# VectorE turns x in 32×32 squares from batch 2 on; folded weights lie by batch in DRAM

## The chip, the core and the metric

One core of a Trainium2 chip runs the whole program. The metric is the device time of one execution in microseconds (us); lower is better. TensorE is called PE here, VectorE DVE, ScalarE ACT, SyncE SP (as in the profile). Every DMA of this kernel is issued by SP, in program order.

## The reference, cut to what matters

```python
# x (8, 8, 512, 64), state (8, 8, 32, 64): batch, head, position, depth
scores  = x @ state.T / 8;   a  = softmax(scores);   xread = a  @ state
scores2 = state @ x.T / 8;   a2 = softmax(scores2);  sread = a2 @ x
t = concat([xread, sread], axis=2)        # 8 * (512 + 32) tokens of 512 values
h = (t @ w1) * (t @ w2)                   # 512 -> 1024, twice
y = (h @ w3) @ w_out                      # 1024 -> 1024 -> 512
h2 = y @ w_in;  out = (h2 - tanh(h2)) @ w_out2     # 512 -> 2048 -> 512
```

The weights arrive as 64-bit numbers, and are turned to fp32 on the chip.

## The kernel before, in words

**First part (about the first 543 us).** `xread` is never formed: the state of a batch is folded into w1 and w2, so that the attention weights are multiplied with folded weights. Nine blocks of tokens (eight batches of 512, one of 256 `sread` rows) go through these stages:

- *Unpacking* (`unpack_abs`, `unpack_tail`, `unpack_clamp`, `unpack_shift`, `unpack_end`, lines 334 to 369): three DVE and one or two ACT operations per piece of weights. `unpack_tail` is on ACT or DVE.
- *w3 times w_out* (`w3_turn`, `w3_mul`): a product of 16 tiles, at the start.
- *Folding* (`fold`, lines 936 to 952): per group r of four batches, pair kk of 128 columns and quarter q, PE multiplies the turned state `uu` with w1 and w2. `fold_whole`, or `fold_hi` and `fold_lo`, take the result out of PSUM into tiles `fe`; `fold_store` (line 976) writes each half j to DRAM (`mdr`), as rows of 1 KB, one store per r, kk, q, half j and, for r = 1, high and low part l.
- *Attention of batch b* (`attn_parts`). `load_xn` brings x with positions on the partitions, as pieces of 64 values (256 bytes). `turn_x` (line 467) turns one quarter q with four PE transposes into PSUM (`x_ps`); `xt` (line 471) copies it out on ACT; `scores` needs all four `xt`. Then softmax both ways on DVE and ACT (`by_head` and `back` are DVE transposes in 32×32 squares, line 493 and 551), `e2t` (PE transposes), `sread`.
- *First product* (`stage1`, tiles `ab_ps`): for batch b and k of 8, the attention weights times the folded weights `m`. `load_m` (line 1057) fetches `m` with four DMAs of 32 partitions; for r = 0 `m_hi` and `m_lo` split it. `ab_take` (ACT) and `ab_mul` (DVE) multiply the two halves, `ab_hi` (ACT) and `ab_lo` (DVE) split the result into `ph`.
- *Second product* (`stage2`, tiles `y_ps`), `y_take` (ACT) and `y_store`, one tile at a time, to DRAM (`ydr`).
- The second model's weights are fetched (`raw_w`), unpacked, and stored to DRAM (`w2dr`) in the same time.

**Second part (from 543 us to the end).** `stage3` (`h_ps`) and `stage4` (`o_ps`) alternate on PE, twelve matmuls each; the `curve` runs on DVE and ACT. The change doesn't touch this part.

**What sets the order.** `part(...)` describes each step with its engine, an estimated duration, needs and buffers. The string `ORDER` (line 91) has a letter for each step: the letter names a stream and an engine. `Plan.run` emits the steps in that order, so each engine's list, and SP's list of DMAs, is written out by the string. Buffers come from rings: four `xt` (shared with `a` and `e2t`), three `m`, four `fe`, two `at`.

An engine does its list strictly in order: what waits holds up what stands behind it. A stage's tiles `m_ps`, `sc_ps` and `sr_ps` are *tiled* matmuls, which use a part of PE's rows or columns; the others use all of it.

Of the kernel before, what the change touches and what calls it, by code (L numbers as in the profile page):

```python
# [68 lines left out]

ENGINES = ("PE", "ACT", "DVE", "SP")  # L70
LETTERS = "abcdefghijklmnopqrstuvwxyzABCDEFGHIJKLMNOPQRSTUVWXYZ0123"
ORDER = (
    "lllllllljljklklljkljklmklnlkjlqjhkkjkjkqkjkkmjknkkjxqkxxkjlkmkxqnkdjkkkqjkkkmkqnkxjkxxqkxjkmjqkk"
    "mknnkqjkkjqkjekqhkfkvqkvkmkmwxmnmxwjqxwlnxkvxqxvxkxkqwwnqwnrkrersrlafgabhsabmhsbmsavqbwvwaqnwbbe"
    "cncvqcfcbhwqbwvgechcadjcqwjkqkcvqkvcmqccncbwqbwvwmfawqnhwbgbebhjcagafcvehhcqccbkvqcfccvghekhagaF"
    "kfbakbebhhgafFmbwmnenwvhgqhwfvwhehwqwfgHhwHehFIqfIghehKfgHhIheqfghhertLsKfgrhrshKzMrALKMLsazMebA"
    "LagfMKhbshbcKcLcbeFMcLacfObchbdMObgHcheIcafgebhOcbhfcKfcgbKcLcceOcfFgfgOhMhcLehMHhacbaFIfOcfczgh"
    "OghhAKhcHeILafKbghfghKzhMhALKLMezFMAfOFfgLgOHhMhIOhHheIKfFfgKgLhhKzMhLhAKHMLIezMAfKfghLgKhLMhhez"
    "MFAfaabgObhfhzOghLAhHMeIafFabgObfhKghhHhOLIOePPKRfRfhKzFMALKgLgheMhzhMfOFALHMOPghfIRahhbKcbPcKLR"
    "cbcOHFcbMaIObdcLcKbgHchKLcbeccafFcObgfIbOFMcOchchOHMhIHKLIMKLgchKcbFMcLKLMOzMALOHMIaacecafKbghfg"  # L80
    "hKLhhKzMALKLMazFMabAebHaFbaIObffOghLghHMOhhIOaebbcFOfcfgObghhcahcOHhcbIbdKcPRcbKcLcPKFPMPKLccLRR"
    "bMORzcMOALMOKHIKLKzMALKLMaFMebLabaMFfcOfcHOhccOIbcHcOccIKgghheLhafFaObbfgKhghhaMFObLHOMhIKHKLIKF"
    "MLKLMKFMHKLILZMZOFMHOLIMaabKbTKLUUTaFMTUbKUbcZTVcKcbcOLFcbcHOHcdLcOITcOTIPaMPKRMbRUbUKbUVLcZLaFM"
    "KbMPUPUORLZcLVOMbRcHcOIcaTcaTUKUcHcbKUFccOTcIZTUVUKMULOZHMVLIFKMLKLMTKTMFUUKUTZTUOFUOULZLMVOMVaa"
    "bbaababKbLKLMaFMTObUcbTUOcTcObULcZTOVMcbacdObUbcOUUcVOZcbTOcPcPRTKcRUUPUaPRKVLZbRbOFMcLKMcKLcTUK"
    "TFMULaULaMVOZccbOcTccTUOUUaabKZbVKFMLKLMKFMTLUKUTMOTFUTUUOLVUZKMVZLKMLKFMLKLMOFMTOTUUKLUMTZKVLUU"
    "TOFMUOVZKLMKTTUUKFLUOMVZOKTTUUOFLULOMZMVOLTMOTUUPKUPRZPVKLRRPTaFMabUaLUObMRbKTTKULUVTUZOMFUOLVMZ"
    "abObccObccOTcTcaOcdbbcbUOUTUTOcVZUbacKbccbUKLccKFMcKLMLKcTFcTMKULUVMLZObFUMOULMZVOcOKTTUUKLUOFML"
    "aTMaVTccZKUUUaObVLZKPPRKFMLaLMaRbabaObTbUKUPPRTKFMTKULUZLMRTKFMULaULMZVbKVbccKFcbcOcbcaKcbbMcKcb"
    "TacbOcTUOcUbUTOcLVZcLDaTEaMOMcLOcLcbUOcTcTcOUMUaObUZbUVbcOcUOVOKTTUUKMDULKEVLMKDMELOMDLEOOOPPRKR"  # L90
    "PPRRKDMLEKMLDEKDMLEKMDLEKDMLEKMDLEKDMLEKMDLEKDMEKDEKDEKDEOFOOLLMOMKLLMMKFOFOOLLMOM333OL3MOOOOOO1"
    "OP2KPR1R3K2LKFMLKLM3PRKPFMLKLMR1OFM2LKM3K1LO2FMOL3MOOK1KL21KFM2LKLM31KM12LOLM32OO112O123O12O23OK"
    "KMLKLMOMLOMOOPPRRPRPR"
)
# [1376 lines left out]
```

## Time and profile before

| | us |
|---|---|
| three runs | 1290.15, 1293.03, 1292.68; median 1292.68 |
| the profiled execution's own time | 1292.19 |
| its span in the trace | 1290.4 |
| PE busy, share of the span | 1275.8, 99% |
| DVE busy | 966.3, 75% |
| ACT busy | 752.6, 58% |
| DMA queue of SP, share of 16 engines | 35.9% |

The profiled execution is one of its own beside the three runs, 0.49 us below their median, and 1.8 us longer than its span. Busy time of PE includes matmuls whose records overlap: a row "x12 | 2.88 us" spans twelve matmuls that start 0.227 us apart. What a group of matmuls costs on PE is the time from its start to the start of what follows it.

### The profile page before, as it was taken

What the parts mean: (1) busy time and instruction counts of PE and PEld (TensorE: products, weight loads), DVE (VectorE), ACT (ScalarE), POOL (GpSimd) and SP (SyncE); (2) the same over time, 40 slices, a digit from 0 to 9 for tenths busy, and PEclk for the clock granted to TensorE, in tenths of its full rate; (3) what the DMA queues carried; (4) which work ended last, traced back from release to release, by engine and by line L of the source; (5) the groups of instructions that cost most, each with busy time, mean ns of one, the idle gap of its engine ahead of it and who ended that gap; (6) DMA issues with size and microseconds to landing.
All of it is one profiled execution on the core that took longest, in us unless ns stands there. A gap on an engine that the chain in (4) does not pass through costs nothing.

```text
span 1290.4 us, 17503 instructions
## 1 busy us (share of the span) xinstructions
PE 1275.8 (99%) x6420; PEld 1017.4 (79%) x6420; DVE 966.3 (75%) x1602; ACT 752.6 (58%) x1208; POOL 0.7 (0%) x6
## 2 busy tenths in 40 slices
PE   8999999999999999999999999999999999999998
PEld 5436777877888799888888888888888888888887
DVE  7888776586757754499787787776877877768777
ACT  8986666486766754465454454554544545545444
POOL 0000000000000000000000000000000000000000
PEclk9999999999999999999999999999999999999999
DMA  9986774577989627530100100100101001001000
GB/s 337 311 257 193 241 236 146 166 216 214 296 267 243 184 74 235 152 120 1 39 27 1 66 1 1 66 1 29 37 1 66 1 1 66 1 1 50 1 34 17
DMA packets 111365, 141.66 MB, mean 110 GB/s; under 512 B 43440, under 2 KB 81328, under 8 KB 109232
## 3 DMA queue, kind: packets, MB, share of 16 engines
q1 hardware_dynamic: 111280, 140.54, 35.9%
q8 instruction: 51, 0.84, 0.3%
q14 instruction: 34, 0.28, 0.1%
HBM read 89.13 MB, written 51.38 MB: 109 GB/s over the span
## 4 chain that ended last, share of the span: by engine, by line
PE 86%; DMA 5%; DVE 3%; ACT 2%; SPq 2%; issue 1%; DVEq 0%; ACTq 0%
PE h_ps L316 27%; PE o_ps L1394 27%; PE ab_ps L316 14%; PE y_ps L1124 14%; DMA raw_p<-in_moe_w_dram 2%; PE m_ps L941 1%; PE m_ps L948 1%; PE x_ps L308 1%; DMA raw<-in_moe_w_dram 1%; DMA mdr<-fe 1%; SPq L758 1%; DMA m<-mdr 1%; PE w3o_ps L790 1%; SPq L753 1%; DMA w2dr_in<-dt_w 1%
## 5 line engine op out<-in xcount | busy, mean ns | idle before, releaser
L316 PE MATMUL h_ps<-yt,w2in 128*128 128x512 f32 (+1 forms) x1728 | 394.0, 377 | 0.0
L316 PEld LDWEIGHTS h_ps<-yt,w2in 128*128 128x128 f32 x1728 | 313.5, 188 | 61.1
L1124 PE MATMUL y_ps<-ph,w3o 128*128 128x512 f32 (+1 forms) x864 | 197.7, 381 | 0.0
L316 PE MATMUL ab_ps<-at,m 128*128 128x512 f32 x768 | 185.1, 393 | 1.0 <-DMA m<-mdr 1.0
L1124 PEld LDWEIGHTS y_ps<-ph,w3o 128*128 128x128 f32 x864 | 153.7, 188 | 32.4 <-issue 3.1
L316 PEld LDWEIGHTS ab_ps<-at,m 128*128 128x128 f32 x768 | 142.5, 188 | 36.5 <-issue 3.3
L1107 DVE TENSOR_TENSOR ac<-ab_ps,ac 128x512 f32<-128x512 f32 (+1 forms) x72 | 47.3, 657 | 36.8 <-PE ab_ps L316 31.7
L286 ACT ACTIVATE ph<-ac 128x512 fp32r<-128x512 f32 (+1 forms) x72 | 43.8, 609 | 48.4 <-DVE ac L1107 34.0
L289 DVE TENSOR_TENSOR ph<-ac,ph 128x512 fp32r<-128x512 f32 (+1 forms) x72 | 47.4, 658 | 27.2 <-ACT ph L286 25.8
L790 PE MATMUL w3o_ps<-wo,w3t 128*128 128x512 f32 x128 | 59.4, 602 | 3.5 <-ACT w3t L286 2.2
L790 PEld LDWEIGHTS w3o_ps<-wo,w3t 128*128 128x128 f32 x128 | 22.7, 190 | 31.7 <-issue 24.4
L286 ACT ACTIVATE ac<-ab_ps 128x512 f32<-128x512 f32 (+1 forms) x72 | 41.2, 572 | 8.3 <-PE ab_ps L316 8.0
L344 ACT ACTIVATE raw_w<-raw_w 128x512 uint16<-128x512 uint32 x32 | 43.9, 1373 | 0.6
L1404 DVE COPY ob<-o_ps 128x512 f32<-128x512 f32 x17 | 11.8, 692 | 39.1 <-PE o_ps L1394 39.1
L286 ACT ACTIVATE fe<-m_ps 128x512 fp32r<-128x512 f32 (+1 forms) x48 | 28.3, 608 | 18.7 <-PE m_ps L941 8.3
L286 ACT ACTIVATE ob<-o_ps 128x512 f32<-128x512 f32 x17 | 10.2, 599 | 45.1 <-PE o_ps L1394 45.1
L335 ACT ACTIVATE dt_w<-raw_w 128x512 f32<-128x512 f32 x32 | 21.5, 673 | 19.3 <-DMA w2dr_in<-dt_w 9.2
L289 DVE TENSOR_TENSOR m<-m 128x512 fp32r<-128x512 f32 x32 | 21.7, 685 | 14.1 <-ACT m L286 14.1
L286 ACT ACTIVATE m<-m 128x512 fp32r<-128x512 f32 x32 | 19.9, 628 | 20.3 <-DMA m<-mdr 20.1
L289 DVE TENSOR_TENSOR fe<-m_ps,fe 128x512 fp32r<-128x512 f32 x32 | 21.3, 687 | 10.3 <-DMA mdr<-fe 5.4
L368 DVE SCALAR_TENSOR_TENSOR dt_w<-raw_w,dt_w 128x512 uint32<-128x512 uint32 x32 | 22.1, 690 | 7.0 <-ACT raw_w L344 5.8
L355 DVE TENSOR_SCALAR dt_w<-dt_w 128x512 f32<-128x512 f32 x32 | 13.4, 420 | 16.8 <-ACT dt_w L335 14.9
(1826 smaller groups left out, 2347.5 us busy)
## 6 DMA issues: line engine op xcount, KB each, us to landing
mdr<-fe SPq DMA_DIRECT2D x96, 256.0 KB, 2.7
m<-mdr SPq DMA_DIRECT2D x128, 128.0 KB, 4.4
raw<-in_moe_w_dram SPq DMA_DIRECT2D x16, 512.0 KB, 9.4
xn<-in_x_dram SPq DMA_DIRECT2D x8, 1024.0 KB, 8.2
m<-mdr SPq DMA_DIRECT2D x128, 64.0 KB, 2.2
ydr<-y SPq DMA_DIRECT2D x32, 256.0 KB, 4.2
raw_w<-in_moe_w_in_dram SPq DMA_DIRECT2D x16, 512.0 KB, 5.4
raw_w<-in_moe_w_out_dram SPq DMA_DIRECT2D x16, 512.0 KB, 4.9
```

Of the source, the lines that this page charges most:

```text
L286: nc.scalar.activation(dst, src, AF.Copy)
L289: nc.vector.tensor_tensor(out=lo, in0=src, in1=hi.bitcast(F32), op=ALU.subtract)
L308: nc.tensor.transpose(dst[:, i * P:(i + 1) * P], s, ident)
L316: nc.tensor.matmul(out_ap, lhs(i), rhs(j), start=(n == 0), stop=(n == m - 1))
L335: nc.scalar.activation(t.bitcast(F32), word(raw, 1).bitcast(F32), AF.Abs)
L344: nc.scalar.activation(tail, word(raw, 0), AF.Copy, scale=TAIL)
L355: nc.vector.tensor_scalar(out=t, in0=t, scalar1=EXP_LO, scalar2=EXP_HI, op0=ALU.max, op1=ALU.min)
L368: nc.vector.scalar_tensor_tensor(out=t if to is None else to, in0=word(raw, 1), scalar=0xC0000007, in1=t, op0=ALU.bitwise_and, op1=ALU.bit ...
L790: nc.tensor.matmul(acc[a], v[:, a * P:(a + 1) * P], wo[:, j].bitcast(F32), start=(j == 0), stop=(j == nj - 1),)
L1107: nc.vector.tensor_tensor(out=ab[b, k], in0=ab[b, k, 1], in1=ab[b, k], op=ALU.mult)
L1124: nc.tensor.matmul(acc[o][:, :n], w3o[k // 4][:, k // 2 % 2, i, c + o * P:c + (o + 1) * P], p[:, j], start=(k == 0 and e == 0), stop=(k == ...
L1394: nc.tensor.matmul(acc[t], g[:, i, t * P:(t + 1) * P], w[:, l, c], start=(f == 0 and e == 0), stop=(f == NF - 1 and e == 2),)
```

## The change

Eight edits, and an order written anew:

1. From batch 2 on, `turn_x` and `xt` are gone. `squares(q)` loads a quarter of x once more from DRAM, already sorted into 32×32 squares (four DMAs, in runs of 32 values, 128 bytes), and `turn_squares(q)` turns all squares of the quarter in one DVE operation in place. `load_xn` stays, for `sread`.
2. `mdr` is laid out by batch: `[l, b, q, n, k, f]`. The rows of a folded tile are now (n b) instead of (b n), because the copy of `uu` interleaves the four batches.
3. `fe` is one tile of 512×2 for both halves j; `fold_store` stores it with one DMA per r, kk, q and l.
4. `load_m` is one DMA over all 128 partitions.
5. For r = 0 `fold_whole` takes both halves on one engine.
6. `y_take` takes two tiles on one engine and `y_store` stores them with one DMA (except for the last two blocks).
7. `part` has an argument `other`: a second engine for the same step. The string `CHOICE` has a bit for each such step; 1 takes the other engine. It applies to `xt`, `take`, `e2take`, `unpack_tail`, the copies of `w3t` and `uu`, `fold_whole`, `ab_take` and `y_take`.
8. Entries of the cost tables, used to make the order.

```diff
-        (r, kk): dram.tile([KT, P, 2, 2, 512], F32, name=f"mdr{r}_{kk}")
+        (r, kk): dram.tile([2, 4, KT, NS, 2, 512], F32, name=f"mdr{r}_{kk}")
...
+    def move(dst, src, eng):
+        if eng == "ACT":
+            copy(dst, src)
+        else:
+            nc.vector.tensor_copy(dst, src)
...
+            def squares(q):
+                s["xt", q] = pt.tile([P, 512], F32, tag="xt", name=f"xt{b}_{q}", bufs=4)
+                for n in range(4):
+                    j, d = divmod(n, 2)
+                    nc.sync.dma_start(
+                        s["xt", q][n * 32:(n + 1) * 32].rearrange("k (c w i) -> k c w i", c=NC, w=4),
+                        x[b, 2 * q + j, :, d * 32:(d + 1) * 32].rearrange(
+                            "(w k c) i -> k c w i", w=4, c=NC
+                        ),
+                    )
+
+            def turn_squares(q):
+                nc.vector.transpose(out=s["xt", q], in_=s["xt", q])
...
+                if b >= SQUARES:
+                    part(
+                        q_s, "SP", "squares", later(squares, q), [(b - 1, "e2t", j) for j in range(G)],
+                        [(b, "xr", q)],
+                        [("xt", (b, "xt", q))],
+                    )
+                    p("DVE", full, turn_squares, (q,), [("xr", q)], [("xt", q)])
+                    continue
...
-        def fold_store(r, kk, q, j, l):
+        def fold_store(r, kk, q, l):
             nc.sync.dma_start(
-                mdr[r, kk][q, :, :, l, j * 256:(j + 1) * 256], fes[r, kk, q, j, l].bitcast(F32)
+                mdr[r, kk][l, :, q].rearrange("b n k f -> n b (k f)"),
+                fes[r, kk, q, l].bitcast(F32).rearrange("p k f -> p (k f)"),
             )
...
-            for q in range(KT):
-                rows = slice(q * NS, (q + 1) * NS)
-                to = mt[b, k][rows].bitcast(F32)
-                of = mdr[r, k // 2][q, bb * NS:(bb + 1) * NS, k % 2]
-                nc.sync.dma_start(*((to, of) if r else (to[:, 1], of[:, 1])))
+            of = mdr[r, k // 2][:, bb, :, :, k % 2].rearrange("l q n f -> (q n) l f")
+            to = mt[b, k].bitcast(F32)
+            nc.sync.dma_start(*((to, of) if r else (to[:, 1], of[:, 1])))
...
-        def ab_take(b, k, n):
+        def ab_take(b, k, n, eng):
             ab[b, k] = pa.tile([P, 512], F32, tag="ac", name=f"ac{b}_{k}")[:, :n]
-            copy(ab[b, k], ab[b, k, 0])
+            move(ab[b, k], ab[b, k, 0], eng)
...
+            if b < B - 1:
+                nc.sync.dma_start(ydr[b][:, os[0]:os[1] + 1, :], ys[b, os])
...
-    "lllllllljljklklljkljklmklnlkjlqjhkkjkjkqkjkkmjknkkjxqkxxkjlkmkxqnkdjkkkqjkkkmkqnkxjkxxqkxjkmjqkk"
+    "ppppppppnpnopoppnopnopqopsnpopnopuohnonoqousnononuoonoBnqBoonduoBorBonuoonooqouoBroBBnuoBnoqoqsu"
```

**PE, in the attention of batch 2.** Names: `x_ps` turned x, `y_ps` second product, `ab_ps` first product, `sc_ps` scores. Before:

```order
242 L308 MATMUL x_ps_2_1543<-ident,xn_1026 128x128 x4
243 L308 MATMUL x_ps_3_1555<-ident,xn_1026 128x128 x4
244 L1124 MATMUL y_ps_0_1011<-ph_6_1413,w3o_875 128x512 x3
245 L1124 MATMUL y_ps_1_1015<-ph_6_1413,w3o_875 128x512 x3
246 L316 MATMUL ab_ps_1_0_1575<-at_1095,m_1_1483 128x512 x6
```

The change, ahead of the same scores:

```order
236 L331 MATMUL ab_ps_0_0_1433<-at_1044,m_0_1376 128x512 x6
237 L1184 MATMUL y_ps_0_899<-ph_7_1401,w3o_784 128x512 x3
238 L1184 MATMUL y_ps_1_903<-ph_7_1401,w3o_784 128x512 x3
239 L527 MATMUL sc_ps_0_1457<-xt_0_1046,uu_359 32x512
240 L527 MATMUL sc_ps_1_1458<-xt_0_1046,uu_359 32x512
```

The groups `x_ps` of four transposes are gone from PE's list from batch 2 on: 32 such groups before, 8 in the change. The scores read `xt`, which DMA and DVE have filled.

**SP, while batch 1 goes through its first product.** Before (`fe` to `mdr` is a fold store, `m` from `mdr` a load of folded weights):

```order
84 L1063 DMA m_0_1380<-mdr_0_94 32x512 x4
85 L978 DMA mdr_1_99<-fe_1_000_1378 256x1x256
86 L978 DMA mdr_1_99<-fe_1_001_1387 256x1x256
87 L978 DMA mdr_1_99<-fe_1_010_1385 256x1x256
88 L978 DMA mdr_1_99<-fe_1_011_1396 256x1x256
```

The change:

```order
76 L491 DMA xn_1537<-in_x_dram 128x32x64
77 L1123 DMA m_4_1550<-mdr_2_96 128x512
78 L1123 DMA m_5_1596<-mdr_2_96 128x512
79 L510 DMA xt_0_1641<-in_x_dram 32x16x32 x4
80 L510 DMA xt_1_1692<-in_x_dram 32x16x32 x4
81 L510 DMA xt_2_1720<-in_x_dram 32x16x32 x4
82 L1031 DMA mdr_1_99<-fe_1_30_1726 32x4x1024
83 L510 DMA xt_3_1750<-in_x_dram 32x16x32 x4
84 L1031 DMA mdr_1_99<-fe_1_31_1748 32x4x1024
85 L1123 DMA m_6_1800<-mdr_3_97 128x512
```

A load of `m` is one row instead of four, a fold store one instead of two, and the four loads of squares of the next batch stand between two loads of `m`.

**DVE, in the same place.** In the change:

```order
271 L518 STREAM_TRANSPOSE xt_0_1641<-xt_0_1641 128x512
272 L518 STREAM_TRANSPOSE xt_1_1692<-xt_1_1692 128x512
273 L304 TENSOR_TENSOR fe_1_31_1748<-m_ps_1_3_0_1711,fe_1_30_1726 128x2x256
274 L304 TENSOR_TENSOR fe_1_31_1748<-m_ps_1_3_1_1712,fe_1_30_1726 128x2x256
275 L518 STREAM_TRANSPOSE xt_2_1720<-xt_2_1720 128x512
276 L1167 TENSOR_TENSOR ac_4_1763<-ab_ps_4_1_1756,ac_4_1763 128x512
277 L304 TENSOR_TENSOR wq_0_1773<-raw_4_388,wq_0_1773 128x512
278 L304 TENSOR_TENSOR ph_4_1777<-ac_4_1763,ph_4_1777 128x512
279 L301 COPY ac_5_1788<-ab_ps_5_0_1766 128x512
```

The turns of squares (L518) stand on DVE between steps of the first product, and some of the copies of `ab_ps` (L301) that ACT did are on DVE.

## Rows read from the trace of the kernel before

**Rows 1.** The page: busy us (share of the span) and instructions by engine.

```profile
PE 1275.8 (99%) x6420; PEld 1017.4 (79%) x6420; DVE 966.3 (75%) x1602; ACT 752.6 (58%) x1208; POOL 0.7 (0%) x6
```

**Rows 2.** Windows: stretch, length, busy by engine, granted clock, DMA share, GB/s.

```profile
0.00:104.00 104.00, 96.04 (x413) 47.68 (x414) 84.26 (x132) 87.28 (x103) 0.70 (x6) 1.00 0.96 296
104.00:450.00 346.00, 344.66 (x2104) 269.30 (x2102) 250.02 (x478) 233.72 (x394) 0.00 (x0) 1.00 0.76 219
450.00:543.00 93.00, 93.00 (x548) 82.85 (x547) 46.49 (x73) 44.70 (x79) 0.00 (x0) 1.00 0.49 146
543.00:1290.00 747.00, 742.08 (x3362) 617.59 (x3360) 585.55 (x921) 386.91 (x635) 0.00 (x0) 1.00 0.08 29
```

**Rows 3.** Waits of PE: who waited for whom, us in total, times, longest.

```profile
PE w3o_ps L790 <- ACT w3t L286: 2.2, 3, 1.4
PE w_ps L308 <- DVE dt_p L368: 2.1, 2, 1.2
PE ab_ps L316 <- DMA m<-mdr: 1.0, 1, 1.0
```

**Rows 4.** Timeline of PE: start us, us, line, tiles, count; two places with `x_ps`.

```profile
154.93 1.09 PE L308 MATMUL x_ps<-ident,xn 128*128 128x128 f32 x8
155.78 3.01 PE L1124 MATMUL y_ps<-ph,w3o 128*128 128x512 f32 x12
158.72 0.96 PE L941 MATMUL m_ps<-wq,uh 64*128 64x512 f32 x6
...
248.31 0.60 PE L308 MATMUL x_ps<-ident,xn 128*128 128x128 f32 x4
248.66 1.62 PE L1124 MATMUL y_ps<-ph,w3o 128*128 128x512 f32 x6
```

**Rows 5.** The chain: start, us, what; two pieces of the second part.

```profile
554.22 2.72 PE o_ps L1394 x12
556.94 2.72 PE h_ps L316 x12
```

**Rows 6.** Groups on DVE up to 544 us: busy us, mean ns of one, idle before.

```profile
L551 DVE STREAM_TRANSPOSE at<-a 128x512 f32<-128x512 f32 x16 | 11.3, 709 | 1.1 <-DVE a L547 0.5
L971 DVE COPY fe<-m_ps 128x512 f32<-128x512 f32 x16 | 11.0, 686 | 3.4 <-PE m_ps L948 3.3
L346 DVE TENSOR_SCALAR raw_p<-raw_p 128x1024 uint16<-128x1024 uint32 x4 | 5.3, 1328 | 0.2 <-ACT dt_p L335 0.2
L346 DVE TENSOR_SCALAR raw_p<-raw_p 128x512 uint16<-128x512 uint32 x4 | 3.0, 741 | 0.3 <-ACT w3f L335 0.3
L1107 DVE TENSOR_TENSOR ac<-ab_ps,ac 128x256 f32<-128x256 f32 x8 | 3.4, 422 | 5.9 <-PE ab_ps L316 5.6
```

**Rows 7.** DMA in the window 278 to 282 us, inside a load of `xn`.

```profile
DMA packets 3693, 0.95 MB, mean 238 GB/s; under 512 B 3690, under 2 KB 3690, under 8 KB 3693
```

**Rows 8.** The page's DMA issues: count, KB each, median us to landing.

```profile
mdr<-fe SPq DMA_DIRECT2D x96, 256.0 KB, 2.7
m<-mdr SPq DMA_DIRECT2D x128, 128.0 KB, 4.4
xn<-in_x_dram SPq DMA_DIRECT2D x8, 1024.0 KB, 8.2
```

**Rows 9.** Tile `m` from 104 to 450 us: its DMAs' time to landing.

```profile
DMA to landing us min/median/max: 1.8/2.8/7.9
```

**Rows 10.** Timeline around 430 us: scores' weight loads, SP's list held up, PE's wait.

```profile
428.84 0.18 PEld L482 LDWEIGHTS sc_ps<-xt,uu 64*32 64x32 f32 x16 [0.35 <-DVE dt_w L360]
...
430.11 3.66 SPq L1242 DMA_DIRECT2D w2dr_out<-dt_w  x2
...
434.16 2.49 SPq L1063 DMA_DIRECT2D m<-mdr  x4
...
437.08 1.63 PE L316 MATMUL ab_ps<-at,m 128*128 128x512 f32 x6 [0.99 <-DMA m<-mdr]
```

More of the change, by code (lines that the diff above doesn't have):

```diff
@@ L389, in tile_kernel, with price, part @@
         plan.ring(name, n)
-    def part(stream, eng, cost, fn, need=(), make=(), take=(), give=(), rank=None, kind="stage"):
+    choice, chosen = iter(CHOICE), [0]
+    def price(cost):
+        if isinstance(cost, tuple):
+            kind, n = cost
+            return COST[kind][0] + COST[kind][1] * n, TAIL_LAG if kind == "tail" else 0.0
+        return cost, 0.0
+    def part(
+        stream, eng, cost, fn, need=(), make=(), take=(), give=(), rank=None, kind="stage",
+        other=None,
+    ):
+        if other is not None:
+            if next(choice, "0") == "1":
+                (eng, cost), other = other, (eng, cost)
+            fn = later(fn, eng)
+            other = (other[0], *price(other[1]), chosen[0])
+            chosen[0] += 1
         size, late = 0, 0.0
@@ L395, in part @@
             cost = size[0]
-        elif isinstance(cost, tuple):
-            kind, n = cost
-            late = TAIL_LAG if kind == "tail" else 0.0
-            cost = COST[kind][0] + COST[kind][1] * n
+        else:
+            cost, late = price(cost)
         stream.append(dict(
-            eng=eng, dur=cost, past=late, fn=fn, need=tuple(need), make=tuple(make),
+            eng=eng, dur=cost, past=late, other=other, fn=fn, need=tuple(need), make=tuple(make),
             take=tuple(t if len(t) == 3 else (*t, 1) for t in take), give=tuple(give), bytes=size, rank=rank,
@@ L607, in sr_lo, with p @@
                 low(xsr[:, q:q + 2], at[B][:, 0, q:q + 2], at[B][:, 1, q:q + 2])
-            def p(eng, cost, f, v=(), need=(), make=(), take=(), give=(), kind="turn"):
+            def p(eng, cost, f, v=(), need=(), make=(), take=(), give=(), kind="turn", other=None):
                 part(
@@ L612, in p @@
                     [(t, (b, *k), u) for t, k, u in take], [(b, *g) for g in give],
-                    rank=3 if b == 0 and eng != "PE" else None, kind=kind,
+                    rank=3 if b == 0 and eng != "PE" else None, kind=kind, other=other,
                 )
@@ L643, in attn_parts @@
                     "ACT", ("scalar", 512), take, (j,), [("scores",)], [("sc", j)], (),
-                    [("sc_ps", j)],
+                    [("sc_ps", j)], other=("DVE", ("vector", 512)),
                 )
@@ L722, in unpack_parts @@
             part(st, "ACT", ("high", n), lambda: unpack_abs(raw(), t()), need, [(key, "abs")], take)
+            ways = {"ACT": ("ACT", ("tail", n)), "DVE": ("DVE", ("vector", n))}
             part(
-                st, tail, ("tail" if tail == "ACT" else "vector", n), lambda: unpack_tail(raw(), tail),
-                [(key, "abs")], [(key, "tail")],
+                st, *ways[tail], lambda eng: unpack_tail(raw(), eng), [(key, "abs")],
+                [(key, "tail")], other=ways["DVE" if tail == "ACT" else "ACT"],
             )
@@ L842, in tile_kernel @@
             part(
-                t3_s, "ACT", ("scalar", 512), lambda t=t: copy(w3v[t], w3x[t]),
-                [("w3x", t)], [("w3t", t)], (), [("w3x", t)],
+                t3_s, "ACT", ("scalar", 512), lambda eng, t=t: move(w3v[t], w3x[t], eng),
+                [("w3x", t)], [("w3t", t)], (), [("w3x", t)], other=("DVE", ("vector", 512)),
             )
@@ L988, in tile_kernel @@
             part(
-                f_s, "ACT", ("scalar", 512), lambda r=r: copy(uu[r][1], uu[r][0]),
-                [("u_ps", r)], [("uu", r)], (), [("u_ps", r)],
+                f_s, "ACT", ("scalar", 512), lambda eng, r=r: move(
+                    uu[r][1].rearrange("p (q n b) -> p q b n", q=KT, b=4),
+                    uu[r][0].rearrange("p (q b n) -> p q b n", q=KT, b=4), eng,
+                ),
+                [("u_ps", r)], [("uu", r)], (), [("u_ps", r)], other=("DVE", ("vector", 512)),
             )
@@ L1149, in tile_kernel @@
                     ([("mh", B, NK - 1, 1)] if b == B - 1 else []) + [
-                        ("mdr", b // 4, k // 2, q, j, l)
-                        for q in range(KT) for j in range(G) for l in range(0 if b >= 4 else 1, 2)
+                        ("mdr", b // 4, k // 2, q, 0, l)
+                        for q in range(KT) for l in range(0 if b >= 4 else 1, 2)
                     ],
@@ L1188, in tile_kernel @@
                         [("ac", *z)], [("ac", ("ac", *z))], [("ab", *z, 0)],
+                        other=("DVE", ("vector", n)),
                     )
```

191 lines of the change are left out of this document (107 added, 84 removed), and 9 rows, old and new, of tables (MOVE, plan).

## The prediction

> **What bounds the kernel now.** I read the engines' busy time first. PE is busy for 1275.8 of 1290.4 us, DVE for 966, ACT for 753 [rows 1]. The windows by stage say where that holds: PE is idle for 8.0 us of the first 104 (104 less 96.0), for 1.3 us of the next 346, and not at all from 450 to 543 [rows 2]. The list of PE's waits names little that a faster engine could remove: 2.2 us for a copy of `w3t` and 2.1 us for unpacked weights at the start, and one wait of 1.0 us for a load of `m` [rows 3]. So PE's own work sets the time, and what leaves PE's list shortens the run, as long as nothing else becomes late. In the second part, 58% of the run, a group of twelve matmuls follows the other every 2.72 us, 0.227 us per matmul [rows 5]; the change doesn't touch it.
>
> **What leaves PE.** The order lists show 32 groups of four `x_ps` transposes before and 8 in the change: 24 go, those of batches 2 to 7. The price of one is read from the timeline, from its start to the start of what follows. A group alone takes 0.35 us (248.31 to 248.66), two in a row 0.85 us (154.93 to 155.78) [rows 4], so one that is followed by another takes 0.50 us. In the list before, the 24 stand in 11 runs: 11 are last in their run, 13 are followed by another. 11 × 0.35 + 13 × 0.50 = 10.4 us. Its lower bound is 24 × 0.35 = 8.4 us, its upper one 24 × 0.50 = 12.0. I take **−10.4 us**. All of it was on the path, since PE had no idle time there.
>
> **New neighbours on PE.** Twelve `y_ps` matmuls ahead of a tiled group take 2.94 us (155.78 to 158.72) [rows 4] against 2.72 us ahead of another full one [rows 5]: entering a tiled group costs about 0.22 us. Counted in the lists, PE goes from a full matmul to a tiled one 36 times before and 38 times in the change (four of the eight `sr_ps` groups are split up into single ones, while some fold groups of r = 0 stand in pairs). I take **+0.4 us**, with bounds of −1 and +1.5.
>
> **Weights with a stride.** `scores` now takes every fourth column of `uu`. The trace has no weight load of this sort. The sixteen loads of one `scores` start within 0.18 us today [rows 10]; the bounds are nothing and a doubling on the path, 8 × 0.18 = 1.4 us. I take **+0.3 us**, near the bottom, because loads overlap matmuls in most of the trace (PEld is busy for 79% of the span beside PE [rows 1]).
>
> **The start.** The first twelve DMAs are the same. The change then loads a second wide piece of w3 before the state, and hands two of the first `w3t` copies to DVE and `unpack_tail` of the first pieces more to ACT. The 4.3 us of waits [rows 3] are short chains of such steps, so they may shrink to nothing (−4) or double (+4). Walking down the new lists with today's durations I find tile 2 of `w3_mul` at the same place, tile 4 a few tenths later, tiles 5 to 7 without the wait for `dt_p`, and a new wait for `dt_p` at about 70 us. I take **−0.5 us**.
>
> **What the work becomes elsewhere, and what hides it.** *DVE* gets 24 turns at 0.709 us = 17.0, 48 more copies of 512 columns net at 0.686 = 32.9 (25 of them `ab_take`), six of 256 columns at 0.422 = 2.5, and 13 tails of 512 columns at 0.741 and four of 1024 at 1.328, less two and one at the start, = 12.1 [rows 6]: 64.5 us in all. ACT loses about as much. Put beside PE's rows in the lists, some 48 us of it fall between 104 and 450 us, where DVE is busy for 250 of 346 us [rows 2]: 298 of 336, or 89%, after. The cover is the 38 us that are left. It is thin, and an engine this full delivers some operands late. I take **+1.0 us** for such waits; the bounds are 0 and the whole gain (first rival).
>
> *ACT* is relieved, which gains nothing, as PE waits for it only at the start. *Fewer, larger DMAs*: 96 fold stores become 48, 256 loads of `m` 64, 36 stores of `y` 22, with the same bytes. A fold store lands in 2.7 us and a load of `m` in about 4.4 today [rows 8], both beside PE's work. The one place where `m` was late is where SP stood for 3.66 us before a store of `w2dr`, with the load of `m` behind it: PE then waited 0.99 us [rows 10]. That wait can go, or come back elsewhere, because SP's list is still in order; I cost the fusions at nothing.
>
> *The squares* are new DMAs: 24 quarters of 256 KB in runs of 128 bytes, 2048 packets each. The trace has none so short. A load of `xn` runs in packets of 256 bytes: 3693 packets in 4 us at 238 GB/s [rows 7], so 1.08 ns per packet over the 16 DMA engines. If a packet of 128 bytes costs as much as one of 256, a quarter takes 2.2 us; if bytes decide, 1.1 us. That is 27 to 53 us of DMA time. From 104 to 450 us the DMA engines are free for 24% of 346 us [rows 2], 83 us, or some 73 when the stretch is 10 us shorter. I take 2.2 us, because the packet's own cost seems to lead already at 256 bytes: 238 GB/s there against a mean of 296 in the first 104 us [rows 2, 7]. It fits, so PE is charged nothing.
>
> The Trainium skill (DMA: Bandwidth & Descriptors, Specifications) says that a transfer needs 512 bytes to run at line rate, and that below that the engine reads, modifies and writes. This rule speaks against the squares; the trace agrees in that the 256-byte load is slower per byte. Taken to its end it is the second rival below, and the sum would be 1297 in place of 1283.
>
> **Sum.** Profiled execution 1292.2 − 10.4 + 0.4 + 0.3 − 0.5 + 1.0 = **1283.0 us**. The profiled execution was 0.5 us below the median of the runs shown (1292.68), which is less than the spread of the three, so I forecast 1283 for the median too.
>
> **Rivals.**
>
> *DVE becomes the bound (no change).* For it: 89% between 104 and 450 us, on an engine that waits in order for PE and ACT by turns; it had 96 us of idle time there before [rows 2]. If half of that idle time, 48 us, can't be used because an operand isn't there yet, the stretch takes 250 + 48 + 48 = 346 us, as before, and the time is 1292. Against it: from 450 to 543 us DVE is busy for half the time [rows 2], and the unpacking of the second model's weights can slide there.
>
> The Trainium skill (VectorE: DVE Perf Modes, Rules for kernel authors) says that a 128×128 transpose belongs on TensorE if its result may land in PSUM, and that DVE is the quickest for 32×32 squares. Read as a rule for this x, it would leave the time at 1292, as this rival does; the first half weighs the operations alone, and the windows show that here PE is the one without room.
>
> *The squares hold up SP's queue (slower).* Place: the loads of the next batch's squares stand in front of loads of `m`, three quarters nearly in a row. Price: if a 128-byte packet costs twice what a 256-byte one does, a quarter takes 4.4 us and three of them 13.3. The ring of three `m` covers two tiles of 24 matmuls, 2 × 24 × 0.227 = 10.9 us [rows 5]. PE loses 2.4 us in each of six batches, 14 us: 1283 + 14 = 1297. It decides from 10.9 / 3 = 3.6 us per quarter, 1.7 times what I take. For it: loads of `m` already land up to 7.9 us after their issue, against a median of 2.8 [rows 9], and one such delay did reach PE [rows 10]. Against it: nothing in the trace costs more per packet for being smaller.
>
> *The start gets better (still faster).* If half of the 8.0 us of PE's idle time goes [rows 2], the time is 1279.
>
> *The change doesn't do what it says.* The lists show the 24 groups gone, so this has no chance of its own.
>
> **Chances.** About 0.2% (2.6 us) is what a measurement of this kernel can tell from no change. The forecast, 1280 to 1287: 0.55. A better start, 1276 to 1280: 0.10. The same gain with more late operands, 1287 to 1290: 0.15. DVE as the bound, 1290 to 1295: 0.11. The queue of squares, about 1297: 0.09. So faster 0.80, same 0.11, slower 0.09. The range that leaves out no more than 2 in 10 is 1277 to 1292.
>
> **What would show it.** `x_ps` with 32 transposes in place of 128, PE idle by no more than 3 us from 104 us to the start of `h_ps`, and that start at about 533 us in place of 543: then the sum holds. DVE over 300 us busy in that stretch and PE's waits naming `ph` or `ac`: the first rival. Waits of PE for `m` with loads of `xt` ahead of them, and squares that take over 3.6 us: the second. If `h_ps` starts near 533 and the total is not 10 us lower, the second part changed, which nothing here foresees.

## The result, and the profile after

| | before | after |
|---|---|---|
| median of the runs, us | 1291.96 (1289.41 to 1293.03, 6 runs) | 1280.64 (1280.09 to 1281.44, 6 runs) |
| ratio to before | | 0.9916, 95% interval 0.9903 to 0.9929 |
| the profiled execution, us | 1292.19 | 1280.81 |
| its span, us | 1290.4 | 1278.7 |

The kernel is 11.3 us faster, and 1283 was forecast for 1280.6. Of the 11.7 us by which the spans differ, 11.25 lie before the first `h_ps`, which starts at 531.93 us instead of 543.18; the second part takes 746.8 us (747.2 before).

The page of the kernel after, part 1, beside [rows 1]:

```profile
PE 1266.8 (99%) x6324; PEld 1008.7 (79%) x6324; DVE 1018.8 (80%) x1694; ACT 695.3 (54%) x1116; POOL 0.7 (0%) x6
```

Its windows by stage, with the columns of [rows 2]; the third stretch ends 1.07 us after the first `h_ps` now starts:

```profile
0.00:104.00 104.00, 98.65 (x440) 50.88 (x441) 94.09 (x145) 84.31 (x101) 0.70 (x6) 1.00 0.92 293
104.00:450.00 346.00, 344.33 (x2028) 266.45 (x2027) 287.84 (x544) 184.64 (x315) 0.00 (x0) 1.00 0.80 233
450.00:533.00 83.00, 83.00 (x504) 74.58 (x503) 51.55 (x87) 41.33 (x68) 0.00 (x0) 1.00 0.57 189
```

Up to `h_ps`, PE's idle time fell from 9.30 us (7.96 + 1.34 + 0) to 7.02 (5.35 + 1.67 + 0), and its busy time from 543.18 − 9.30 = 533.88 to 531.93 − 7.02 = 524.91. So about 9.0 us are work that is gone, and 2.3 us are waits that are gone. All of the second came at the start: 7.96 to 5.35.

PE's waits after, the first rows:

```profile
PE u_ps L323 <- DMA zst<-in_state_dram: 1.7, 1, 1.7
PE w3o_ps L844 <- DVE wo L383: 1.7, 2, 1.4
...
PE ab_ps L331 <- ACT m L295: 0.8, 1, 0.8
PE w3o_ps L844 <- ACT w3t L295: 0.5, 1, 0.5
```

The 2.1 us for `dt_p` of [rows 3] are gone, and the 2.2 us for `w3t` are 0.5. A new one, 1.7 us for the state (`zst`), took some of it back.

Two rows of the page's DMA issues after, beside [rows 8]: half as many fold stores, and one transfer for each `m` (the row has the half of them that is 512 KB); each lands later than one of its smaller forerunners did.

```profile
mdr<-fe SPq DMA_DIRECT2D x48, 512.0 KB, 3.3
m<-mdr SPq DMA_DIRECT2D x32, 512.0 KB, 6.1
```

Now the new work. DMA in the window 288 to 290 us of the kernel after, in which almost nothing but squares moves:

```profile
DMA packets 1589, 0.21 MB, mean 105 GB/s; under 512 B 1585, under 2 KB 1585, under 8 KB 1588
...
q1 hardware_dynamic: 1588, 0.20, 69.0%
```

16 engines × 2.0 us × 0.69 / 1588 = 13.9 ns of an engine per packet of 128 bytes. A quarter of 2048 packets thus takes 2048 × 13.9 / 16 = 1.8 us of all engines, between the two bounds of the prediction (1.1 and 2.2). But the same place in the timeline, on SP, shows a second price:

```profile
282.82 10.46 SPq L510 DMA_DIRECT2D xt<-in_x_dram  x12
293.37 0.57 SPq L1123 DMA_DIRECT2D m<-mdr  x1
```

Three quarters, twelve loads, hold SP's list for 10.46 us, 3.5 us per quarter: twice what their packets need. The load of `m` behind them is issued only then. The prediction had priced the packets, and not SP's time. The experiments show what SP's time is worth.

### The profile page after: what moved, and what is told of

Its sections match the earlier page's. It is cut to its first block, busy times and chain, and to the rows that moved or that the text cites. A ratio compares the mean times of both kernels' runs of the same rounds, so it can differ in the third digit from the quotient of the medians.

```text
span 1278.7 us, 16949 instructions
## 1 busy us (share of the span) xinstructions
PE 1266.8 (99%) x6324; PEld 1008.7 (79%) x6324; DVE 1018.8 (80%) x1694; ACT 695.3 (54%) x1116; POOL 0.7 (0%) x6
## 4 chain that ended last, share of the span: by engine, by line
PE 92%; DVE 3%; DMA 2%; SPq 1%; ACT 1%; issue 0%; DVEq 0%; ACTq 0%
PE h_ps L331 28%; PE o_ps L1468 27%; PE ab_ps L331 15%; PE y_ps L1184 14%; PE w3o_ps L844 3%; PE m_ps L1002 1%; PE m_ps L995 1%; DMA raw_p<-in_moe_w_dram 1%; DMA zst<-in_state_dram 1%; PE sc_ps L527 1%; PE sr_ps L621 1%; PE et_ps L323 0%; DMA m<-mdr 0%; DVE h_ps L1440 0%; SPq L470 0%; SPq L807 0%
## 5 line engine op out<-in xcount | busy, mean ns | idle before, releaser
L295 ACT ACTIVATE ph<-ac 128x512 fp32r<-128x512 f32 (+1 forms) x72 | 44.1, 612 | 64.2 <-DVE ac L1167 50.0
L295 ACT ACTIVATE ac<-ab_ps 128x512 f32<-128x512 f32 (+1 forms) x43 | 24.5, 571 | 16.7 <-PE ab_ps L331 16.3
L304 DVE TENSOR_TENSOR fe<-m_ps,fe 128x512 fp32r<-128x512 f32 x32 | 20.5, 680 | 8.9 <-DMA mdr<-fe 8.1
L359 ACT ACTIVATE raw_w<-raw_w 128x512 uint16<-128x512 uint32 x19 | 26.1, 1374 | 0.5
L295 ACT ACTIVATE at<-at 128x512 fp32r<-128x512 f32 x16 | 10.1, 631 | 27.2 <-DVE r L557 21.6
```

The costliest lines, as they stand in the source:

```text
L304: nc.vector.tensor_tensor(out=lo, in0=src, in1=hi.bitcast(F32), op=ALU.subtract)
L359: nc.scalar.activation(tail, word(raw, 0), AF.Copy, scale=TAIL)
```

## The experiments

Theory at the outset: the columns of the 24 `x_ps` groups are the gain, and DVE and the DMA engines have room for what replaces them; fusions and choice of engine give next to nothing. Rivals: the gain comes from the new order and the choice of engines; or DVE or SP is about to become the bound. All times below are medians; "slower by" is against the kernel after, 1280.64 us. The kernel before, timed again beside each of them, had medians from 1290.57 to 1291.96 us, so such a difference is uncertain by about 1 us. An undisturbed second part of 746.7 to 747.2 us stands in each of these profiles, so every difference arose before `h_ps`.

### pe_more: the 24 groups given back to PE, unused

```diff
             def scores():
                 for j in range(G):
                     s["ps", j] = ps(f"sc_ps{b}_{j}")
+                for q in range(KT if b >= SQUARES else 0):
+                    transposes(s["ps", q % 2], [ident] * 4)
```

> The changed kernel with 24 more groups of four transposes on TensorE, of the identity into the score banks just before the scores of batches 2 to 7, one group per quarter; nothing reads them, the scores overwrite them. It gives TensorE back the columns of the 24 x_ps groups and nothing else. Theory (a group taken from TensorE is worth its own 0.44 us, as the kernel before showed 10.5 us for 24): about 1280.6 + 10.5 = 1291 us. Rival (most of the gain is the new order and the choice of engines, and TensorE had room beside the groups): at most 1287 us.

Measured: 1291.25 us (ratio to the kernel before 1.0004, 0.9995 to 1.0013), slower by 10.6. The theory stands: taking 24 groups off PE is worth 10.6 us in this order, 0.44 us each, and that is nearly the whole change of 11.3. Its `h_ps` starts at 542.91 us, 10.98 later.

### x_on_pe and x_on_pe2: x turned on PE again, in the new order

The loads of squares are left out, and where DVE turned, PE turns and ACT copies. No place in PE's banks is planned for it, so a free bank is borrowed: in the first run the one freed first, in the second the one freed last.

```diff
...
-                nc.vector.transpose(out=s["xt", q], in_=s["xt", q])
+                k = min((m[0][1], i) for i, m in enumerate(plan.banks) if not m[0][0])[1]
+                xp = pw.tile([P, 512], F32, tag=f"ps{k}", name=f"x_ps{b}_{q}")
+                transposes(xp, [xn[b][:, c, q * P:(q + 1) * P] for c in range(NC)])
+                copy(s["xt", q], xp)
```

> The changed kernel with its new order, but x of batches 2 to 7 is turned by PE again, four transposes per quarter into a free PSUM bank, copied out by ScalarE, where the change has DVE turn the squares; no squares are loaded. My theory (PE's list sets the time, the 24 groups are worth 10.4 us): about 1291 us, 9 to 12 above the changed kernel. Rival (the new order, the engines chosen and the fewer DMAs brought the gain, and the squares little): under 1285.

> The changed kernel with x of batches 2 to 7 again turned on TensorE and copied by ScalarE, in the change's own order, and without the squares' loads; unlike x_on_pe the group goes into the free bank that was freed last, so that the next step of TensorE does not ask for that bank at once. Theory (x_on_pe lost 10.5 us to the columns and about 10 us to waits for the bank it borrowed): the waits for the copies of x fall below 3 us, and the time is 1291 to 1294 us. Rival (in this order any turning on TensorE costs over 20 us, because ScalarE is late there): 1300 us or more, with the same waits for xt.

Measured: 1303.37 us (ratio 1.0091, 1.0074 to 1.0107) and 1296.98 (1.005, 1.0033 to 1.0066). PE's waits in the first:

```profile
PE ab_ps L331 <- ACT xt L295: 6.9, 10, 0.7
```

and in the second:

```profile
PE ab_ps L331 <- ACT xt L295: 2.0, 3, 0.7
```

Together with the rows for `st_ps` and `m_ps` (1.4 us each) the first lost 9.7 us in waits for the copy out of its borrowed bank; the second lost 2.3, and the time fell by 6.4. Both are above what was expected. The second is 16.3 us slower than the kernel after: 10.6 are the groups; PE's idle time from 104 to 450 us rose by 3.9 (346 − 340.47 = 5.53 against 1.67). Some 2 us I could not attribute. An order that was written for one set of steps punishes another one put in its place; this pair says little more.

### before_squares: only the squares, in the old order

```diff
             def turn_x(q):
+                if b >= 2:
...
+                    s["xt", q] = pt.tile([P, 512], F32, tag="xt", name=f"xt{b}_{q}", bufs=4)
...
+                    return
             def xt(q):
+                if b >= 2:
+                    nc.vector.transpose(out=s["xt", q], in_=s["xt", q])
+                    return
```

The squares are loaded where PE turned, by the four loads of the change.

> The kernel before in its old order; only the transposes of x from batch 2 on are replaced: the four loads of squares are issued where PE's transposes stood, and DVE turns them where ScalarE copied. All else is as before. My theory: PE's list gets 10.4 us shorter, but the squares are loaded late, so DVE stands some 2 to 3 us per quarter for them and gives a part back: 1283 to 1290. Rival (without the new order the squares cost what they save): 1291 or more.

Measured: 1361.36 us (ratio 1.0534, 1.0508 to 1.0560). The expectation missed by 70 us. PE's waits:

```profile
PE sc_ps L497 <- DVE xt L485: 21.0, 10, 6.0
PE sc_ps L497 <- DVE ac L1122: 9.5, 1, 9.5
```

and DVE's own:

```profile
DVE xt L485 <- DMA xt<-in_x_dram: 86.0, 24, 8.9
```

DVE waited 24 times out of 24 for squares, up to 8.9 us, with everything of its list behind. In the kernel after DVE waits for squares twice, 0.9 us in all. From the issue of a quarter's last load to its turn the records show 2.7 us at the median here, about the landing alone, and 5.5 us in the kernel after. So the squares need their loads ahead of the turns, and the new order gives them that. What else of the change this run lacks (the fusions, the choices) has a part of the loss that it doesn't tell apart. And nearly a third of the loss is PE's granted clock:

```profile
104.00:450.00 346.00, 308.19 (x1626) 223.95 (x1625) 218.05 (x404) 181.27 (x306) 0.00 (x0) 0.93 0.73 197
```

The mean is 0.93 here, at the lower level of 1.2 GHz in part, where the kernels before and after have 1.00. Summed over PE's busy stretches up to `h_ps`, that is an estimated 22 us.

### before_dmas2: only the data's way, in the old order

Layout by batch, one load per `m`, one store per fold for both halves j, `y` in pairs, strided `uu`; x stays on PE. The ring `fe` has two of the large buffers here, as in the change: a first version (before_dmas) had four, and for that SBUF has no room: 16.375 KB per partition were left for a pool of 24.

```diff
-            f = fes[r, kk, q, j, l] = pt.tile(
-                [P, 2, 256], F32R if r else F32, tag="fe", name=f"fe{r}_{kk}_{q}{j}{l}", bufs=4
-            )
+            if (r, kk, q, l) not in fes:
+                fes[r, kk, q, l] = pt.tile(
+                    [P, 2, 512], F32R if r else F32, tag="fe", name=f"fe{r}_{kk}_{q}{l}", bufs=2
+                )
...
-                y = pt.tile([P, 512], F32, tag="fe", name=f"y{b}_{o}", bufs=4)
+                    ys[b, "pair", o // 2] = pt.tile([P, 2, 512], F32, tag="fe", name=f"y{b}_{o}", bufs=2)
```

> The kernel before, with its own order and x turned on TensorE, and of the change only the data's way: the folded weights by batch in DRAM, one load per m, one store per fold and half, y rows in pairs, and the weights of the scores strided. Theory (the fusions and the stride cost and give next to nothing): 1290.5 to 1293.5 us. Rival (the fewer transfers take waits out of the order before): 1289 us or less.

Measured: 1299.05 us (ratio 1.0066, 1.0051 to 1.0081): 8.5 us slower than the kernel before, timed beside it at 1290.57. The theory (nothing) fell. One place does nearly all of it. Its timeline, SP, DVE and PE:

```profile
179.34 0.33 SPq L1156 DMA_DIRECT2D ydr<-y  x1
182.14 0.69 DVE L289 TENSOR_TENSOR fe<-m_ps,fe 128x512 fp32r<-128x512 f32 x1 [6.22 <-DMA ydr<-y]
...
182.88 3.35 PE L316 MATMUL ab_ps<-at,m 128*128 128x512 f32 x7 [5.31 <-DVE fe L289]
```

and its window from 180 to 190 us:

```profile
180.00:190.00 10.00, 7.12 (x20) 5.59 (x21) 6.06 (x11) 2.33 (x5) 0.00 (x0) 0.66 0.18 66
```

Folds and `y` share the ring `fe`. Two large buffers have taken the place of four small ones, and a pair of `y` rows keeps one until its second row is computed and the store has landed. DVE waited 6.22 us for it, PE 5.31, and after that pause PE's granted clock was 0.66 in the mean of this stretch, partly the lower level of 1.2 GHz: 10 × 0.34 = 3.4 us more at most, 3.0 while PE was busy. 5.3 + 3.0 is about the 8.5 that were lost. The fusion makes a buffer live longer here; with the old order it is no gain at all.

### old_engines, old_start, old_late: the choice of engines taken back

The order stays, and the steps of `CHOICE` run on their first engine again: all of them; only those of the first weights and of batches 0 and 1; only the later ones, with which all `ab_take` and `y_take` count. The edit of the first, in the branch for steps that `CHOICE` moves:

```diff
-            fn = later(fn, eng)
+                fn = later(fn, other[0])
+            else:
+                fn = later(fn, eng)
```

> The changed kernel in its new order, but every step that can choose its engine runs on the engine it had by default, mostly ScalarE, at the same place of the program. DVE loses some 48 us of work, ScalarE gains about as much. My theory: the PE list is the same, most of the copies have slack, within 3 us of the changed kernel, 1280 to 1284, most of the loss at the start where ScalarE is full. Rival (moving copies off ScalarE made the gain): 1287 or more.

> The changed kernel in its own order, with the choice of engine taken back only for the steps of the start: copies and tails of the first weights (w3t, xt, uu, the folds of whole tiles) and the pieces of batches 0 and 1. Theory (of the 8.7 us that old_engines lost, the part before 104 us came from VectorE and ScalarE being late with the first weights): 3 to 5 us slower than the changed kernel, 1284 to 1286 us, with the waits for dt_p, w3f and wo back on TensorE and h_ps starting 3 to 5 us later. Rival (the loss came from the middle): at most 1.5 us slower.

> The changed kernel in its own order, with the choice of engine taken back only for the steps behind the start: the takes of ab, y, scores and e2 of batches 2 to 7 and the tails of the second model's weights. Theory (the rest of the 8.7 us of old_engines): 3.5 to 5.5 us slower than the changed kernel, 1284 to 1286 us, and with old_start together about 8.7 us. Rival (the two halves lean on each other: once the start is late the later steps are early enough, or the other way round): together under 6 us or over 12 us.

Measured: 1289.30 us (ratio 0.9984, 0.9975 to 0.9994), 1290.24 (0.9999, 0.9990 to 1.0008) and 1283.40 (0.9941, 0.9927 to 0.9954): slower by 8.7, 9.6 and 2.8. My expectation for the first (at most 3.4 us) fell, and that for the second too: it loses 9.6, not 3 to 5; the third lost a little less than the 3.5 expected. The two halves do not add up (12.4 against 8.7). That is the rival's sign that they lean on each other, but only 0.4 us past the 12 it had named, which is inside the uncertainty. Windows of old_start, which lost most of it by 134 us:

```profile
50.00:80.00 30.00, 26.61 (x116) 11.29 (x115) 24.80 (x38) 26.01 (x31) 0.00 (x0) 1.00 1.02 304
80.00:104.00 24.00, 22.21 (x103) 10.31 (x101) 18.53 (x31) 18.61 (x25) 0.00 (x0) 1.00 0.44 170
104.00:114.00 10.00, 9.20 (x50) 4.43 (x48) 6.91 (x12) 5.09 (x9) 0.00 (x0) 1.00 0.43 172
114.00:124.00 10.00, 7.64 (x36) 4.67 (x33) 8.19 (x14) 5.51 (x11) 0.00 (x0) 1.00 0.81 210
124.00:134.00 10.00, 10.00 (x72) 7.11 (x72) 8.31 (x18) 4.32 (x8) 0.00 (x0) 0.83 0.61 157
```

and the first two of these windows in the kernel after:

```profile
50.00:80.00 30.00, 30.00 (x170) 13.32 (x155) 29.02 (x44) 26.41 (x33) 0.00 (x0) 1.00 1.07 326
80.00:104.00 24.00, 24.00 (x100) 11.70 (x99) 23.51 (x40) 15.63 (x27) 0.00 (x0) 1.00 0.51 197
```

From 50 to 104 us PE is never idle in the kernel after, and idle for 3.39 + 1.79 = 5.2 us without the choices, in waits for `dt_p` (two, 2.8 us), `fe` and others; DVE is busy for 52.5 of these 54 us in the one and for 43.3 in the other. The choices taken back are some 25 steps: DVE had five of the 16 copies of `w3t`, four of eight `xt`, four tails of `raw`, two `sc` and one `uu`; ACT had three tails of `raw_p` and six folds. They matter because unpacking alternates between ACT and DVE, each in order. DVE's waits of old_start from 45 to 104 us, the first rows, name ACT in the middle of such chains:

```profile
DVE raw L384 <- ACT raw L360: 2.6, 2, 1.8
DVE dt L371 <- ACT dt L351: 2.3, 3, 1.8
```

The same list of the kernel after has 0.8 us in all, none of it for ACT. Then, in old_start, come 0.80 + 2.36 us of idle time and, behind the longest wait (2.36 us, for `ph`), a granted clock of 0.83 in ten microseconds, 1.7 us more. In the kernel before, PE was idle for 2.43 us from 50 to 104 us; so the new order without the choices is worse at the start than the old one, and with them better.

### dve_more: 48 more copies on DVE

```diff
                 nc.vector.transpose(out=s["xt", q], in_=s["xt", q])
+                nc.vector.tensor_copy(s["xt", q], s["xt", q])
+                nc.vector.tensor_copy(s["xt", q], s["xt", q])
```

> The changed kernel with two copies of each turned quarter onto itself behind its transpose on VectorE: 48 more VectorE instructions of about 0.7 us, 33 us in all, VectorE then at about 321 of 346 us between 104 and 450 us. Theory (VectorE has little room left, and each quarter turned comes later): slower than the changed kernel by 3 to 10 us, with waits for ac, ph or fe on TensorE. Rival (the squares are turned early enough and VectorE still has room): at most 1.5 us slower.

Measured: 1284.09 us (ratio 0.9954, 0.9939 to 0.9969), slower by 3.4. Its window:

```profile
104.00:450.00 346.00, 342.54 (x2012) 263.84 (x2011) 304.10 (x587) 181.93 (x312) 0.00 (x0) 1.00 0.79 231
```

A copy from SBUF to SBUF took 0.43 us, not the 0.7 that I had from copies out of PSUM, so only 20.5 us were added. DVE at 304 of 346 us (88%) costs 3.4 us, at the low end of what was expected. PE's idle time here rose from 1.67 to 3.46, in waits for `fe` and `ac` and none for `xt`; the rest is busy time that I could not attribute. That is the load that the prediction expected of the change itself (298 of 336, 89%, priced at +1.0 us). DVE is not the bound there; in this run a microsecond more on it cost 0.17 in the mean (3.4 / 20.5).

### squares_twice: each load of squares issued twice

```diff
-                for n in range(4):
+                for n in (0, 1, 2, 3, 0, 1, 2, 3):
```

> The changed kernel with each of the 96 loads of squares issued twice, to the same place: 40 us more of the sixteen DMA engines' time (1.66 us per quarter by the measured 13 ns per packet of 128 bytes) and 96 more issues on SyncE's queue, between 104 and 450 us. Theory (there was room on the DMA engines and on the queue): at most 2 us slower than the changed kernel. Rival (SyncE's queue, in which m and the weights stand behind the squares, becomes late): 5 us slower or more, with waits of TensorE for m, xn or raw weights from DMA.

Measured: 1359.90 us (ratio 1.0535, 1.0521 to 1.0550), slower by 79. The theory that there was room fell. PE's waits:

```profile
PE ab_ps L331 <- ACT m L295: 28.3, 5, 9.8
PE ab_ps L331 <- DMA m<-mdr: 13.0, 2, 10.5
PE sc_ps L527 <- DVE xt L518: 6.3, 2, 4.2
```

and SP's timeline:

```profile
187.09 18.94 SPq L510 DMA_DIRECT2D xt<-in_x_dram  x24
...
206.75 5.86 SPq L510 DMA_DIRECT2D xt<-in_x_dram  x8
...
213.34 1.40 SPq L1123 DMA_DIRECT2D m<-mdr  x2
```

For 26 us SP issues hardly anything but squares, and `m` comes late, just as the second rival of the prediction had it. But the run alone does not say why: twice the issues, twice the packets, and the second write of a place waits for the first (SP stood 22.6 us for that). Its window says two things more:

```profile
104.00:450.00 346.00, 295.44 (x1602) 221.93 (x1601) 237.29 (x442) 145.36 (x256) 0.00 (x0) 0.92 0.75 206
```

The DMA engines were less busy here than in the kernel after (0.75 against 0.80), so they were not full. And PE's granted clock, 0.92 in the mean, is by the same estimate 19 us of the 79; most of the rest is idle time. The next run takes the issues alone.

### m_in_four: each `m` loaded by four transfers again

```diff
-            nc.sync.dma_start(*((to, of) if r else (to[:, 1], of[:, 1])))
+            for q in range(KT):
+                rows = slice(q * NS, (q + 1) * NS)
+                t4, o4 = to[rows], of[rows]
+                nc.sync.dma_start(*((t4, o4) if r else (t4[:, 1], o4[:, 1])))
```

> The changed kernel with one thing undone: each m is again loaded by four transfers of 32 rows instead of one, the same bytes from the same place. That adds 192 issues to SyncE's queue, which by the kernel before (256 issues, 107 us of its queue) are 72 us more; the queue's issues then take about 335 of the 532 us before h_ps, where the changed kernel has 262 and squares_twice had 322 of 609. Theory (what squares_twice ran out of was SyncE's queue, which issues one transfer after the other in a fixed order, and the fused loads and stores are what makes room in it for the squares): slower than the changed kernel by 5 us or more, with waits of TensorE for m, fe or xt. Rival (squares_twice lost its time to the bytes and to the second write into a tile that waits for the first, and the fused loads give nothing): at most 1.5 us slower.

Measured: 1303.83 us (ratio 1.0079, 1.0056 to 1.0103), slower by 23 (the four runs lie between 1298.70 and 1304.82). Bytes, order and everything else are those of the kernel after; only SP has 192 issues more. The theory that the fused loads make room on SP stands, and the rival that they give nothing falls. PE's waits, the first row:

```profile
PE ab_ps L331 <- DMA m<-mdr: 5.4, 3, 2.7
```

and the window:

```profile
104.00:450.00 346.00, 329.85 (x1879) 249.04 (x1864) 268.58 (x499) 169.17 (x293) 0.00 (x0) 0.99 0.82 220
```

PE is idle for 16.2 us here (1.67 in the kernel after), in many waits of 0.2 to 2.7 us for `m`, its copies, `fe` and `ac`. This doesn't settle squares_twice: SP's issues took less time there (322 us up to `h_ps`, against 348), and the loss was three times as large. There the squares stand in blocks, with the second writes standing for the first, and PE's waits are up to 10.5 us with a lower clock behind them; how the 79 us divide stays open.

How far SP runs ahead is best read from SP's own waits: how long it stands, before a load of `m`, for PE to give a buffer of `m` free. Each is one row of SP's waits from 104 to 530 us (us, times, longest). Before:

```profile
SPq L1063 <- PE ab_ps L316: 60.6, 32, 5.2
```

before_dmas2, the fusions alone:

```profile
SPq L1069 <- PE ab_ps L316: 117.9, 42, 7.2
```

The kernel after:

```profile
SPq L1123 <- PE ab_ps L331: 64.2, 29, 6.5
```

squares_twice:

```profile
SPq L1123 <- PE ab_ps L331: 38.7, 15, 6.5
```

m_in_four:

```profile
SPq L1126 <- PE ab_ps L331: 17.6, 18, 3.8
```

This is the ledger of the change on SP. The fusions nearly double the time in which SP is ahead of PE (60.6 to 117.9), and the kernel with the squares has 64.2 left. Without the fused loads it is 17.6. Summing the records of SP's issues up to `h_ps` says the same: 285 us in 513 issues before, 161 in 259 with the fusions alone, 262 in 355 after (76 of them the 96 loads of squares), 348 in 547 with `m` in four. A record can hold a part of the wait before it, so these sums are upper bounds. The slack doesn't rank every run: squares_twice has more of it than m_in_four and lost more.

### squares_from_1: batch 1 by squares too

```diff
+                if b == 0:
+                    for q in ((0,), (1, 2, 3))[j]:
+                        load_squares[1](q)
```

Four more groups leave PE; batch 1's squares are loaded behind each half of batch 0's `back`.

> The changed kernel with batch 1 turned in squares on VectorE as well, its squares loaded behind the rows of batch 0 that go back: four more x_ps groups leave TensorE. Theory (a group is worth 0.44 us, and batch 1 comes behind 60 us, where VectorE is 97% busy but the first scores wait for weights): 1.0 to 2.0 us faster than the changed kernel, 1278.6 to 1279.6 us. Rival (at the start VectorE and the DMA engines are full, and the squares come late): slower than the changed kernel by 1 us or more.

Measured: 1289.39 us (ratio 0.9988, 0.9979 to 0.9997), slower by 8.8; the rival's number stands, and its reason in part. SP's timeline:

```profile
67.18 11.00 SPq L518 DMA_DIRECT2D xt<-in_x_dram  x4
...
80.19 8.96 SPq L518 DMA_DIRECT2D xt<-in_x_dram  x12
...
89.88 1.42 SPq L1136 DMA_DIRECT2D m<-mdr  x2
```

The first two `m` are issued at 89.88 us instead of 84.02. Most of the first row is no issuing, but SP standing for a buffer, as its waits from 60 to 104 us show:

```profile
SPq L518 <- PE sr_ps L634: 8.9, 1, 8.9
```

PE's waits show `m` and `fe`:

```profile
PE m_ps L1015 <- ACT fe L295: 3.9, 2, 3.6
PE st_ps L323 <- DMA m<-mdr: 3.8, 1, 3.8
```

Behind them the granted clock was 0.74 from 90 to 100 us and 0.92 from 100 to 110, which by the same estimate is 1.8 of the 8.8 us.

No run here beats the kernel after. Loading batch 1's squares at another place of SP's list wasn't tried.

## Why the prediction was right, and where it was not

**PE bounds, and columns off PE's list are time.** Right, and shown by pe_more: 10.6 us for 24 groups. From start to start the 24 groups of the kernel before took 10.49 us, with one wait of 0.35 us among them, so −10.4 was the right size. The row with that wait:

```profile
306.79 1.09 PE L308 MATMUL x_ps<-ident,xn 128*128 128x128 f32 x8 [0.35 <-DVE ac L1107]
```

**Neighbours and stride.** Forecast +0.7 together. PE's busy time fell by 8.97 us where the groups without their wait were 10.14, so all else on it grew by 1.2. The stride is a small part. The kernel after shows one group of scores, and what follows it:

```profile
416.36 0.24 PEld L527 LDWEIGHTS sc_ps<-xt,uu 64*32 64x32 f32 x16 [0.36 <-issue]
416.36 1.12 PE L527 MATMUL sc_ps<-xt,uu 64*32 64x512 f32 x16
417.40 1.66 PE L331 MATMUL ab_ps<-at,m 128*128 128x512 f32 x6
```

Sixteen loads take 0.24 us against 0.18 [rows 10]; the shortest such group before another takes 1.047 us against 1.019 from start to start, 8 × 0.028 = 0.2 us in all (forecast +0.3).

**The start** is the term that was mis-sized: forecast −0.5, measured −2.6 (PE's idle time up to 104 us, 7.96 to 5.35). It makes up nearly all of the 2.4 us between forecast and result, and is the third rival (half of the 8.0 us, −4) come true in part. "ACT is relieved, which gains nothing, as PE waits for it only at the start" is the step that failed: old_start shows that the choices at the start alone hold 9.6 us in this order. I took the choices for a shift of load between two engines with room; but the order is written around them, and they decide when the chains that alternate between ACT and DVE come to their end. How much of the 2.6 us is the choices and how much the new order was not tested.

**Late operands**, +1.0: PE's idle time from 104 us to `h_ps` rose from 1.34 to 1.67, or from 0.99, +0.7, if the 0.35 is counted with the groups. So counted, the terms give the whole: −10.49 + 1.18 − 2.61 + 0.68 = −11.24 us, against 11.25 measured at the start of `h_ps`. DVE was busy for 287.84 us there, not 298; over the whole run it got 52.5 us more (966.3 to 1018.8), not 64.5. With 304 (dve_more) the price is 3.4 us. So the first rival's place was right and its price too high: even at that load the loss is 3.4 us, not the whole gain.

**"I cost the fusions at nothing."** The sum came out, but the step is wrong. Alone, in the old order, they cost 8.5 us (before_dmas2); and taking one of them out of the new one costs 23 (m_in_four). They are worth nothing by themselves, and in this order the squares gain nothing without the fused `m`.

**"It fits, so PE is charged nothing."** True of this order, but by another resource than the one reckoned. I weighed 27 to 53 us of the DMA engines against 73 us of room; the packets took 24 × 1.8 = 43. SP's list was not in the sum: 96 issues, 76 us in all (0.64 us at the median, 0.79 in the mean). The second rival named the place (loads of `m` behind three quarters of squares), and gave 3.6 us per quarter as the point from which it decides. Three quarters in a row took 10.46 us on SP at 282.82 us, 3.5 each, and 11.27 at 400.50, 3.8 each, and PE did not wait behind either. The forecast was lucky here: a price that it had left out came to the rival's own limit. In squares_twice `m` is late behind the squares, as the rival said.

The Trainium skill (DMA: Bandwidth & Descriptors, Issuing engines are not separate DMA queues) says that the time an engine's sequencer needs to start a DMA is usually small beside the DMA itself. In the trace of this kernel it is not: a load of squares holds SP for 0.64 us and lands in 3.1 (medians), and twelve in a row held it for 10.46. The Trainium skill (DMA: Bandwidth & Descriptors, Rules for kernel authors) says to use one transfer over 128 partitions instead of two over halves of them; m_in_four, with four over quarters, agrees: it is 23 us slower.

The other rule weighed, that transfers under 512 bytes run below line rate (the Trainium skill, DMA: Bandwidth & Descriptors, Specifications), holds in direction here: 16 × 128 bytes / 13.9 ns is 147 GB/s while the engines are busy, against 238 with 256-byte packets [rows 7]. But a packet of 128 bytes costs less than one of 256, and not twice as much, as the second rival had needed: 13 ns against 18 by the medians of the records.

## What to carry to other kernels

Where one engine is busy for 99%, work taken off its list is worth its own time from start to start, and the forecast is decided by what the replacement does to the engines and queues that run in order beside it. Price a new DMA three times: its packets, the time to landing, and the time that its issue holds the queue, with what stands behind it; and read the queue's slack also from how long it waits for buffers. Edits that are worth nothing alone (fused transfers, a step on the other engine) can be what pays for the one that gains, so cost them with it and not one by one.
